# Attention turns of a fused attention and two-MLP kernel in another order

## The chip, the core and the metric

One NeuronCore of a Trainium2 chip. The metric is the device time of one execution in microseconds (us); less is better. The engines named below each run their own list of instructions in order: TensorE (PE; its weight loads are listed apart as PEld), VectorE (DVE), ScalarE (ACT), GpSimd (POOL) and SyncE (SP), which here only issues transfers.

## What is computed

Attention over 4 batches of 12 heads (448 positions of 64 numbers, float32), with q and k normalised by their root mean square and a gain; its result, as 1792 rows of 768, goes through two gated MLPs.

```
def _attn_ref(q, k, v, g_q, g_k):
    q_n, k_n = (rmsnorm(q, g_q), rmsnorm(k, g_k))
    scores = scale * np.matmul(q_n, k_n.transpose(0, 1, 3, 2))
    scores = scores - np.max(scores, axis=-1, keepdims=True)
    attn = np.exp(scores)
    attn = attn / (np.sum(attn, axis=-1, keepdims=True) + 1e-09)
    return np.matmul(attn, v)
...
x = _moe_ref(x)     # (x @ w_a) * (x @ w_b) @ w_out
x = _moe2_ref(x)    # sigmoid(x @ w_gate) * (x @ w_val) @ w_out
```

## The kernel before

Attention takes two heads (a pair) at a time, 24 pairs in all. The work is a software pipeline written out by hand: the tuple `turns` lists steps as (function, offset of the pair, arguments), and a loop over i runs the list once for each turn, every step on pair i + offset. Nothing reorders it: each engine gets its instructions in the order of that list. `begin`, `first` (turn 1) and `end` are such lists for the start and the finish; `turns` runs for i = 2 to 22, 21 times. The MLPs follow, with their own planner, which the change leaves alone; a few of their steps (`decode`, which unpacks weights on ACT and DVE, and `early_hi`, `early_lo`) run inside the turns.

What a turn does, with the names that the trace shows:

- Scores: `s(0, t)`, L350, for t = 0 to 3. Keys and queries are split into a high and a low half (KH, KL, QH, QL), so each score tile is three matmuls. For t = 0, 1, 2 two heads' tiles of 64 rows run side by side, for t = 3 one of 128 rows. Seven score tiles s, in a ring of four PSUM banks.
- Maxima and exponentials: `top`, L356, is the negated row maximum on DVE (tile nm); `exp`, L368, the exponential with the row sum on ACT (tile P, or P3 for t = 3). A score tile's bank is free after its `exp`.
- Turning the exponentials: `x_tr(-1, j, z)`, L378, L381 and for j = 3 L383 to L386, transposes P of the pair of the turn before into a PSUM tile tr. `x_out(-1, j, z)` copies that tile to pt: with z = 0 on ACT (L397, 512 columns, 448 for j = 3), with z = 1 on DVE (L395, 384 columns).
- Value products: `pv(i, part)`, L410, eight matmuls a part, in four concurrent couples, into the one bank pv. Part 0 takes pt of j = 0 and 1, part 1 that of j = 2 and 3; part 1 runs a turn later, as `pv(-2, 1)`. `norm(-2)`, L445 on DVE, then scales pv by the reciprocals rs into xs, and `put` writes xs to DRAM.
- The reciprocals' row: `rsum` on DVE (L417, L418) makes rc; `rsum_tr` (L424) transposes it into a tr tile; `rsum_post` (L429 on ACT, then a transfer from SP) writes it to DRAM; `rsum_get` reads it back three times, spread over partitions, as rs.
- The next pairs' queries and keys: `squares` and `scale` on POOL, `mean` (L239, L253) and `newton` (L268 to L270) on DVE, `rsqrt` on ACT; `t_tr(2, 1)` and `t_tr(2, 0)`, L303 to L308, transpose them into tr tiles; `k_hi` (L323), `k_lo` (L333), `q_hi` (L313), `q_lo` (L318) make the halves; `k_ends` copies 64 columns on POOL.

All tr tiles, ten in a turn, share one ring of three PSUM banks: a tile takes the bank of the one three before it and has to wait until that one was read out.

```
ps_tr = actx.enter_context(tc.tile_pool(name="ps_tr", bufs=3, space=bass.MemoryType.PSUM))
ps_v = actx.enter_context(tc.tile_pool(name="ps_v", bufs=1, space=bass.MemoryType.PSUM))
```

Of the kernel before, what the change touches and what calls it, by code (L numbers as in the profile page):

```python
# [23 lines left out]
def attention_then_two_gated_mlps(  # L24
# [90 lines left out]
    def attention():  # L115
# [269 lines left out]
            for c in range(3):  # L385
                nc.tensor.transpose(tr[:, 64 + P * c:64 + P * c + P], p[c][:, NQ:NQ + P], ident)  # L386

        def x_out(i, j, z):
            d = st[i]
            if z == 0:  # L390
                d["pt"][j] = pt.tile([P, S if j == R else S2], F32, tag=f"pt{j == R}", name="pt", bufs=2 if j == R else 4)
            w = slice(0, S) if j == R else slice(512 * z, S2 if z else 512)
            tr = d.pop(("X", j, z))[:, 0:w.stop - w.start]
            if z:
                nc.vector.tensor_copy(d["pt"][j][:, w], tr)  # L395
            else:
                nc.scalar.copy(out=d["pt"][j][:, w], in_=tr)  # L397
# [102 lines left out]
        def warm(i, n):  # L500
# [17 lines left out]

        first = (
            (s, 0, 0), (x_tr, -1, 0, 0), (x_tr, -1, 0, 1), (s, 0, 1), (top, 0, 0), (x_out, -1, 0, 0), (exp, 0, 0),  # L520
            (top, 0, 4), (exp, 0, 4), (mean, 2), (x_out, -1, 0, 1), (t_tr, 1, 1), (t_tr, 1, 0), (top, 0, 1),
            (k_hi, 1), (load, 4), (load_r, 3), (load_v, 1), (k_lo, 1), (q_hi, 1), (rsqrt, 2), (q_lo, 1), (k_ends, 1),
            (exp, 0, 1), (top, 0, 5), (newton, 2), (scale, 2, 1), (scale, 2, 2), (scale, 2, 0), (s, 0, 2),
            (x_tr, -1, 1, 0), (x_out, -1, 1, 0), (exp, 0, 5), (rsum, -1),
            (x_tr, -1, 1, 1), (x_out, -1, 1, 1), (s, 0, 3),
            (x_tr, -1, 2, 0), (top, 0, 2), (x_out, -1, 2, 0), (exp, 0, 2), (x_tr, -1, 2, 1), (rsum_tr, -1), (top, 0, 6), (exp, 0, 6),
            (x_out, -1, 2, 1), (rsum_post, -1), (pv, -1, 0), (top, 0, 3), (t_tr, 2, 1), (exp, 0, 3), (mean, 3), (rsqrt, 3), (x_tr, -1, 3, 0),
            (k_hi, 2), (newton, 3), (k_lo, 2), (t_tr, 2, 0), (x_out, -1, 3, 0), (q_hi, 2), (q_lo, 2), (k_ends, 2),
        )

        turns = (
            (rsum_get, -2), (early, 0), (put, -3), (s, 0, 0), (s, 0, 1),
            (x_tr, -1, 0, 0), (x_tr, -1, 0, 1), (top, 0, 0), (x_out, -1, 0, 0), (exp, 0, 0), (top, 0, 4),
            (exp, 0, 4), (x_out, -1, 0, 1), (pv, -2, 1), (scale, 2, 1), (scale, 2, 0), (scale, 2, 2), (top, 0, 1),
            (exp, 0, 1), (load, 4), (load_r, 3), (load_v, 1), (x_tr, -1, 1, 0), (top, 0, 5), (rsum, -1), (exp, 0, 5),
            (x_out, -1, 1, 0), (x_tr, -1, 1, 1), (norm, -2), (x_out, -1, 1, 1), (s, 0, 2),
            (s, 0, 3), (decode, 0, 0), (early_hi, -1), (squares, 3), (early_lo, -1), (x_tr, -1, 2, 0),
            (top, 0, 2), (x_out, -1, 2, 0), (exp, 0, 2), (x_tr, -1, 2, 1), (rsum_tr, -1), (top, 0, 6), (exp, 0, 6), (x_out, -1, 2, 1), (rsum_post, -1),
            (pv, -1, 0), (top, 0, 3), (t_tr, 2, 1), (exp, 0, 3), (decode, 0, 1), (mean, 3), (rsqrt, 3), (x_tr, -1, 3, 0),
            (k_hi, 2), (newton, 3), (k_lo, 2), (t_tr, 2, 0), (x_out, -1, 3, 0), (q_hi, 2), (q_lo, 2), (k_ends, 2),  # L540
        )

        end = (
            (close, -1), (rsum_get, -3), (put, -4), (s3, -1, fetch_third, 0), (s, -1, 0), (s, -1, 1),
            (x_tr, -2, 0, 0), (x_tr, -2, 0, 1), (top, -1, 0),
            (exp, -1, 0), (rsum, -2), (x_out, -2, 0, 0), (top, -1, 4), (exp, -1, 4), (x_out, -2, 0, 1), (pv, -3, 1),
            (top, -1, 1), (exp, -1, 1), (x_tr, -2, 1, 0), (top, -1, 5), (x_out, -2, 1, 0), (x_tr, -2, 1, 1),
# [816 lines left out]
    with tc.manual_schedule():  # L1364
        main = mlps()
        attention()
        open_places(6, 4, 2, 3)
        begin_mm("mm1", 2)
        for c in range(KC):
            place(where[0]["A22"], "l", c, F32, "f")  # L1370
        for n, c in (("A22", 0), ("A21", 0), ("A22", 1), ("A21", 1), ("A21", 2), ("A22", 2)):
            stage_in(0, n, c)
        for c in range(KC):
            stage_in(0, "A11", c)
        low_third(1)
        sum_third(2)
        next(main)
        cast_third(2)
        next(main)
        next(main)  # L1380
        low_third(2)
        ready[0] = True
        for _ in main:
            pass
# [29 lines left out]
```

## Time and profile before

| | |
|---|---|
| time, 3 runs | 1216.91 us median (1214.32 to 1217.16) |
| profiled execution | 1218.25 us; span 1216.5 us, 1.75 us around it |
| busy share of the span | PE 98%, PEld 84%, DVE 76%, ACT 54%, POOL 13% |
| chain that ended last, by engine | PE 89%, DVE 5%, DMA 2%, ACT 2% |
| stretch 120 to 150 us: busy of 30 us | PE 30.00, DVE 26.09, ACT 22.98, POOL 17.70; granted clock 1.00 |

The span is the time from the first to the last instruction of the profiled execution. The chain follows the work that ended last back in time, at each step to what released it. A matmul's end is modelled, so a PE that is busy all the time says only that its instructions follow one another closely; where the time goes is read from the distances between starts.

### The profile page before, as it was taken

The numbers are of one execution on the slowest core, as the hardware profiler recorded it, in microseconds if no ns is written. First come the engines' busy times: TensorE is split into PE (matmuls) and PEld (weight loads), VectorE is DVE, ScalarE is ACT, GpSimd is POOL, SyncE is SP. The second block draws the span as 40 slices with busy tenths as digits, with TensorE's granted clock in tenths as the row PEclk, the third lists the DMA queues.
The fourth block names the chain that finished last, engine by engine and source line by source line (L and its number), as shares of the span: only waits on it lengthen the run. The fifth ranks groups of instructions, "written<-read, shape, count | busy, mean of one in ns | idle before, by whom it ended". The sixth has DMA issues, their size and how long they took to land.

```text
span 1216.5 us, 18277 instructions
## 1 busy us (share of the span) xinstructions
PE 1197.6 (98%) x6468; PEld 1016.2 (84%) x6468; DVE 918.7 (76%) x1625; ACT 654.0 (54%) x1276; POOL 157.3 (13%) x241
## 2 busy tenths in 40 slices
PE   8999999999999999999999999999999999999997
PEld 6666666667888888888888888888888888999997
DVE  8888888977858687875768688876786877666672
ACT  7778778864533433444355566534545344445542
POOL 5665668600000000000000000000000000000000
PEclk9999999999999999999999999999999999999999
DMA  5444455348235464654955753234665654777683
GB/s 134 133 141 118 121 149 161 95 147 307 61 113 182 140 204 148 199 187 132 326 183 184 242 178 117 77 125 126 183 194 144 204 160 143 266 254 238 197 258 97
DMA packets 142764, 205.78 MB, mean 169 GB/s; under 512 B 23208, under 2 KB 116560, under 8 KB 142672
## 3 DMA queue, kind: packets, MB, share of 16 engines
q1 hardware_dynamic: 142064, 204.18, 53.5%
q8 instruction: 51, 0.84, 0.3%
q10 hardware_dynamic: 480, 0.43, 0.1%
q14 instruction: 41, 0.34, 0.1%
q0 software_dynamic: 128, 0.00, 0.0%
HBM read 150.21 MB, written 54.35 MB: 168 GB/s over the span
## 4 chain that ended last, share of the span: by engine, by line
PE 89%; DVE 5%; DMA 2%; ACT 2%; issue 1%; POOL 0%; ACTq 0%; SPq 0%; DVEq 0%; POOLq 0%
PE mm L992 46%; PE mm L1275 13%; PE mm L1285 10%; PE pv L410 7%; PE s L350 6%; PE tr L381 4%; PE tr L303 1%; PE tr L378 1%; DVE xl L627 1%; DMA wd<-d 1%; DMA fh<-xd 1%; PE tr L386 1%; DMA xd<-xs 0%; DVE u L1016 0%; DVE al L904 0%
## 5 line engine op out<-in xcount | busy, mean ns | idle before, releaser
L992 PE MATMUL mm<-xl,wh 128*128 128x512 f32 (+1 forms) x1008 | 370.3, 367 | 3.6 <-DVE xl L627 3.6
L992 PE MATMUL mm<-xh,wh 128*128 128x512 f32 (+1 forms) x1008 | 369.6, 367 | 2.4 <-ACT u L1044 2.4
L992 PE MATMUL mm<-xh,wl 128*128 128x512 f32 (+1 forms) x1008 | 371.4, 369 | 0.0
L992 PEld LDWEIGHTS mm<-xl,wh 128*128 128x128 f32 x1008 | 190.6, 189 | 27.6 <-DVE xl L627 4.8
L992 PEld LDWEIGHTS mm<-xh,wh 128*128 128x128 f32 x1008 | 190.7, 189 | 26.8 <-ACT u L1044 2.7
L992 PEld LDWEIGHTS mm<-xh,wl 128*128 128x128 f32 x1008 | 190.4, 189 | 21.1
L627 DVE TENSOR_TENSOR wl<-d,wh 128x384 fp32r<-128x384 f32 x250 | 136.5, 552 | 67.0 <-ACT wh L1152 41.2
L813 ACT CAST wh<-d 128x384 fp32r<-128x384 f32 x166 | 82.0, 514 | 98.1 <-DVE d L801 75.1
L700 DVE SCALAR_TENSOR_TENSOR d<-d,raw 128x384 uint32<-128x384 uint32 x138 | 77.8, 564 | 55.3 <-ACT d L693 49.4
L693 ACT ACTIVATE d<-raw 128x384 f32<-128x384 f32 x138 | 75.6, 553 | 80.6 <-DMA raw<-in_moe_w_out_dram 40.5
L368 ACT ACTIVATE P<-s,nm 128x448 f32<-128x448 f32 x168 | 105.0, 635 | 4.4 <-DVE nm L356 3.6
L1152 ACT CAST wh<-d 128x384 fp32r<-128x384 f32 x84 | 43.2, 514 | 118.3 <-issue 36.8
L356 DVE TENSOR_REDUCE nm<-s 128x1 f32<-128x448 f32 x168 | 97.5, 614 | 3.1 <-PE s L350 3.1
L1285 PE MATMUL mm<-wh,gh 128*128 128x384 f32 x294 | 98.8, 336 | 0.7 <-ACT al L1300 0.4
L1285 PE MATMUL mm<-wl,gh 128*128 128x384 f32 x294 | 98.6, 335 | 0.0
L1285 PE MATMUL mm<-wh,gl 128*128 128x384 f32 x294 | 98.5, 335 | 0.0
L1275 PE MATMUL mm<-gl,wh 128*128 128x512 f32 x252 | 92.6, 368 | 0.0
L1275 PE MATMUL mm<-gh,wl 128*128 128x512 f32 x252 | 92.4, 366 | 0.0
L1275 PE MATMUL mm<-gh,wh 128*128 128x512 f32 x252 | 91.7, 364 | 0.0
L696 DVE SCALAR_TENSOR_TENSOR raw<-raw 128x384 uint32<-128x384 uint32 x140 | 78.4, 560 | 4.0
L397 ACT COPY pt<-tr 128x512 f32<-128x512 f32 x96 | 54.9, 572 | 47.8 <-PE tr L381 45.2
L1062 DVE TENSOR_TENSOR u<-mm,u 128x896 f32<-128x896 f32 x48 | 52.2, 1087 | 30.3 <-PE mm L992 30.2
(161 smaller groups left out, 1947.5 us busy)
## 6 DMA issues: line engine op xcount, KB each, us to landing
gd<-u SPq DMA_DIRECT2D x60, 448.0 KB
u<-gd SPq DMA_DIRECT2D x60, 448.0 KB
d<-wd SPq DMA_DIRECT2D x132, 192.0 KB
raw<-in_moe_w_out_dram SPq DMA_DIRECT2D x48, 384.0 KB
wd<-d SPq DMA_DIRECT2D x72, 192.0 KB
raw<-in_moe_w_a_dram SPq DMA_DIRECT2D x24, 384.0 KB
raw<-in_moe_w_b_dram SPq DMA_DIRECT2D x24, 384.0 KB
raw<-in_moe_w_val_dram SPq DMA_DIRECT2D x23, 384.0 KB
```

Source lines behind the costliest of these rows:

```text
L350: nc.tensor.matmul(out_, w[e, o:o + P], x[e, m:m + S], start=(n == 0), stop=(n == 2))
L356: nc.vector.tensor_reduce(out=d["nm"][:, t:t + 1], in_=d["ps"][t], axis=AX.X, op=ALU.max, negate=True)
L368: nc.scalar.activation(out=e, in_=d["ps"].pop(t), func=AF.Exp, bias=d["nm"][:, t:t + 1], accum_out=d["sum"][:, t:t + 1])
L410: nc.tensor.matmul(d["pv"][64 * h:64 * h + 64], w, x, start=(j == 0), stop=(j == R), skip_group_check=True)
L627: eng.tensor_tensor(out=lo, in0=t, in1=f32(hi), op=ALU.subtract)
L693: nc.scalar.activation(out=f32(t), in_=f32(high), func=AF.Copy, scale=2.0 ** -112)
L696: nc.vector.scalar_tensor_tensor(out=low, in0=high, scalar=0x80000000, in1=low, op0=ALU.bitwise_and, op1=ALU.bitwise_or)
L700: nc.vector.scalar_tensor_tensor(out=t, in0=t, scalar=3, in1=low, op0=ALU.logical_shift_left, op1=ALU.bitwise_or)
L813: nc.scalar.copy(out=hi, in_=t)
L992: nc.tensor.matmul(ps[:, o:o + size], w[:, P * c:P * c + P], x[:, o:o + size], start=(p in (1, 5) and c == 0 and z == 0), stop=(c == KC - ...
L1275: nc.tensor.matmul(ps[:, o:o + size], w[:, P * un:P * un + P], g[:, o:o + size], start=(p in (1, 5) and f == 0 and z == 0), stop=(f == HF ...
L1285: nc.tensor.matmul(ps[:, o:o + HB], g[:, P * t:P * t + P], w, start=(p in (1, 5) and f == 0 and z == 0), stop=(f == HF - 1 and z == 2), sk ...
```

## The change

`turns` is laid out anew, `first` and `end` in the two steps that cross a turn's edge, and `x_out` gets a switch that exchanges its two engines.

- `pv(-2, 1)` stands right behind `s(0, 0)` and `s(0, 1)`, and `pv(-1, 0)` right behind `s(0, 2)` and `s(0, 3)`. The transposes that stood between them come after.
- `rsum`, `rsum_tr` and `rsum_post` move from the end of the turn to its first third; `rsum_get` now runs in the same turn, not at the start of the next.
- `q_lo` moves to the next turn, behind `rsum`.
- `x_out` of j = 2 has its engines exchanged: z = 0 (512 columns) goes to DVE, z = 1 (384 columns) to ACT. Maxima, exponentials and the other copies take other places.

```
@@
-        def x_out(i, j, z):
+        def x_out(i, j, z, swapped=False):
...
-            if z:
+            if bool(z) != swapped:
                 nc.vector.tensor_copy(d["pt"][j][:, w], tr)
@@
-            (k_hi, 2), (newton, 3), (k_lo, 2), (t_tr, 2, 0), (x_out, -1, 3, 0), (q_hi, 2), (q_lo, 2), (k_ends, 2),
+            (k_hi, 2), (newton, 3), (k_lo, 2), (t_tr, 2, 0), (x_out, -1, 3, 0), (q_hi, 2), (k_ends, 2), (rsum_get, -1),
@@
         turns = (
-            (rsum_get, -2), (early, 0), (put, -3), (s, 0, 0), (s, 0, 1),
-            (x_tr, -1, 0, 0), (x_tr, -1, 0, 1), (top, 0, 0), (x_out, -1, 0, 0), (exp, 0, 0), (top, 0, 4),
...
+            (early, 0), (put, -3), (s, 0, 0), (s, 0, 1), (pv, -2, 1), (top, 0, 0), (exp, 0, 0), (top, 0, 4), (exp, 0, 4),
+            (rsum, -1), (q_lo, 1), (rsum_tr, -1), (rsum_post, -1), (scale, 2, 1), (scale, 2, 0), (scale, 2, 2),
...
+            (x_out, -1, 1, 1), (load, 4), (load_r, 3), (load_v, 1), (rsum_get, -1), (s, 0, 2), (s, 0, 3), (pv, -1, 0),
...
+            (x_out, -1, 2, 0, True), (t_tr, 2, 1), (x_out, -1, 2, 1, True), (rsqrt, 3), (x_tr, -1, 3, 0), (k_hi, 2),
@@
-            (close, -1), (rsum_get, -3), (put, -4), (s3, -1, fetch_third, 0), (s, -1, 0), (s, -1, 1),
+            (close, -1), (put, -4), (s3, -1, fetch_third, 0), (s, -1, 0), (s, -1, 1),
```

On PE, in one turn, from the end of `s(0, 1)` to the start of `s(0, 2)` (L410 is `pv`, L378 and L381 are `x_tr`, L424 is `rsum_tr`):

```order
 L350 MATMUL s<-KL,QH 128x448 x2
-L378 MATMUL tr<-ident,P_1361 128x2x64
-L381 MATMUL tr<-ident,P 128x128 x6
 L410 MATMUL pv<-pt,v 64x448 x2
 L410 MATMUL pv<-pt,rz_281 64x448 x2
-L378 MATMUL tr<-ident,P_1361 128x2x64
+L424 MATMUL tr<-ident,rc 7x128
+L378 MATMUL tr<-ident,P_1356 128x2x64
+L381 MATMUL tr<-ident,P 128x128 x6
+L378 MATMUL tr<-ident,P_1356 128x2x64
 L381 MATMUL tr<-ident,P 128x128 x6
 L350 MATMUL s<-KH,QH 128x448 x2
```

Seven transposes left the place ahead of `pv` and stand behind it; with `rsum_tr` that makes 15 transposes in a row.

On PE, in the same turn, from the end of `s(0, 3)` to `t_tr(2, 1)` (L303):

```order
 L350 MATMUL s<-KL,QH 128x448
-L378 MATMUL tr<-ident,P_1361 128x2x64
-L381 MATMUL tr<-ident,P 128x128 x6
-L424 MATMUL tr<-ident,rc 7x128
 L410 MATMUL pv<-pt,v 64x448 x4
+L378 MATMUL tr<-ident,P_1356 128x2x64
+L381 MATMUL tr<-ident,P 128x128 x6
 L303 MATMUL tr<-ident,qkn 128x128 x3
```

Here too the seven transposes went behind `pv`, where the ones of `t_tr` and `x_tr(-1, 3, 0)` follow: 21 in a row.

On DVE, the second half of a turn of before, from the maxima of `s(0, 2)` on:

```order
L356 TENSOR_REDUCE nm<-s 128x1 x2
L395 COPY pt<-tr 128x384
L356 TENSOR_REDUCE nm<-s 128x1
L694 TENSOR_SCALAR raw<-raw 128x384
L239 TENSOR_REDUCE ms<-sq 128x14
L253 TENSOR_SCALAR ms<-ms 128x14
L268 SCALAR_TENSOR_TENSOR t<-y 128x14
```

and a turn's second half of after, in a turn with two steps of `decode` (L696 and L700):

```order
L395 COPY pt<-tr 128x384 x2
L696 SCALAR_TENSOR_TENSOR raw<-raw 128x384
L356 TENSOR_REDUCE nm<-s 128x1 x3
L700 SCALAR_TENSOR_TENSOR d_1697<-d_1697,raw 128x384
L239 TENSOR_REDUCE ms<-sq 128x14
L253 TENSOR_SCALAR ms<-ms 128x14
L395 COPY pt<-tr 128x512
L268 SCALAR_TENSOR_TENSOR t<-y 128x14
```

The copy of `x_out(-1, 2, .)` on DVE moved from between the maxima to behind `mean` (L239, L253), and is the one of 512 columns now.

## Rows read from the trace of the kernel before

**Rows 1.** Chain that ended last: start us, us, what; first and last regular turn

```profile
30.76 1.43 PE s L350 x12
...
245.04 1.42 PE s L350 x12
```

**Rows 2.** Timeline, PE: start us, us, line, op, out<-in, count; one turn

```profile
148.55 0.47 PE L350 MATMUL s<-KH,QH 64*128 64x448 f32 x2
...
149.47 0.37 PE L350 MATMUL s<-KH,QL 64*128 64x448 f32 x2
149.67 0.37 PE L350 MATMUL s<-KL,QH 64*128 64x448 f32 x2
149.97 0.33 PE L378 MATMUL tr<-ident,P 128*128 128x128 f32 x1
150.13 0.82 PE L381 MATMUL tr<-ident,P 128*128 128x128 f32 x6
150.88 0.97 PE L410 MATMUL pv<-pt,v 128*64 128x448 f32 x4
...
152.54 0.33 PE L378 MATMUL tr<-ident,P 128*128 128x128 f32 x1
152.70 0.82 PE L381 MATMUL tr<-ident,P 128*128 128x128 f32 x6
...
154.76 0.36 PE L350 MATMUL s<-KL,QH 128*128 128x448 f32 x1
154.97 0.27 PE L378 MATMUL tr<-ident,P 128*128 128x128 f32 x1
...
155.73 0.27 PE L424 MATMUL tr<-ident,rc 128*7 128x128 f32 x1
155.93 1.72 PE L410 MATMUL pv<-pt,v 128*64 128x448 f32 x8
```

**Rows 3.** Timeline, PE, after the turns: an MLP matmul, then value products

```profile
274.41 0.34 PE L992 MATMUL mm<-xl,wh 128*128 128x384 f32 x1
274.58 0.34 PE L992 MATMUL mm<-xh,wl 128*128 128x384 f32 x1
274.85 0.97 PE L410 MATMUL pv<-pt,v 128*64 128x448 f32 x4
```

**Rows 4.** Timeline, same turn as Rows 2: ACT's first copy, PE's weight loads

```profile
150.66 0.58 ACT L397 COPY pt<-tr 128x512 f32<-128x512 f32 x1 [1.15 <-PE tr L381]
...
152.59 0.69 PEld L381 LDWEIGHTS tr<-ident,P 128*128 128x128 f32 x6
```

**Rows 5.** Timeline near the end: PE waits for a bank that ACT reads

```profile
267.75 0.58 ACT L397 COPY pt<-tr 128x512 f32<-128x512 f32 x1 [0.60 <-PE tr L381]
...
268.39 0.33 PE L378 MATMUL tr<-ident,P 128*128 128x128 f32 x1 [0.29 <-ACT pt L397]
...
268.56 0.49 PE L381 MATMUL tr<-ident,P 128*128 128x128 f32 x3
```

**Rows 6.** Groups by shape, 30 to 255 us: count, busy us, mean ns, idle before

```profile
L395 DVE COPY pt<-tr 128x384 f32<-128x384 f32 x63 | 34.8, 552 | 3.9 <-PE tr L381 3.4
...
L318 DVE TENSOR_TENSOR QL<-tr,QH 128x512 fp32r<-128x512 f32 x21 | 14.5, 692 | 4.7 <-ACT QH L313 4.7
...
L239 DVE TENSOR_REDUCE ms<-sq 128x14 f32<-128x448 f32 x19 | 11.8, 619 | 0.0
...
L700 DVE SCALAR_TENSOR_TENSOR d<-d,raw 128x384 uint32<-128x384 uint32 x8 | 5.4, 680 | 0.0
...
L696 DVE SCALAR_TENSOR_TENSOR raw<-raw 128x384 uint32<-128x384 uint32 x8 | 4.6, 576 | 0.0
```

**Rows 7.** Timeline, DVE, same turn as Rows 2

```profile
151.68 1.14 DVE L356 TENSOR_REDUCE nm<-s 128x1 f32<-128x448 f32 x2
152.74 0.16 DVE L417 TENSOR_SCALAR rc<-sum 128x7 f32<-128x7 f32 x1
...
153.11 0.62 DVE L445 TENSOR_TENSOR xs<-pv,rs 128x448 f32<-128x448 f32 x1
```

More of the change, by code (lines that the diff above doesn't have):

```diff
@@ L534, in attention @@
[L534 to L538, printed above, removed]
@@ L539, in attention @@
-            (pv, -1, 0), (top, 0, 3), (t_tr, 2, 1), (exp, 0, 3), (decode, 0, 1), (mean, 3), (rsqrt, 3), (x_tr, -1, 3, 0),
-            (k_hi, 2), (newton, 3), (k_lo, 2), (t_tr, 2, 0), (x_out, -1, 3, 0), (q_hi, 2), (q_lo, 2), (k_ends, 2),
+            (early, 0), (put, -3), (s, 0, 0), (s, 0, 1), (pv, -2, 1), (top, 0, 0), (exp, 0, 0), (top, 0, 4), (exp, 0, 4),
+            (rsum, -1), (q_lo, 1), (rsum_tr, -1), (rsum_post, -1), (scale, 2, 1), (scale, 2, 0), (scale, 2, 2),
+            (x_tr, -1, 0, 0), (x_out, -1, 0, 0), (top, 0, 1), (exp, 0, 1), (x_tr, -1, 0, 1), (norm, -2),
@@ new lines, in attention @@
+            (x_tr, -1, 1, 0), (x_out, -1, 1, 0), (top, 0, 5), (exp, 0, 5), (x_tr, -1, 1, 1), (x_out, -1, 0, 1),
+            (x_out, -1, 1, 1), (load, 4), (load_r, 3), (load_v, 1), (rsum_get, -1), (s, 0, 2), (s, 0, 3), (pv, -1, 0),
+            (decode, 0, 0), (early_hi, -1), (squares, 3), (early_lo, -1), (top, 0, 2), (exp, 0, 2), (top, 0, 6),
+            (exp, 0, 6), (x_tr, -1, 2, 0), (x_tr, -1, 2, 1), (top, 0, 3), (exp, 0, 3), (decode, 0, 1), (mean, 3),
+            (x_out, -1, 2, 0, True), (t_tr, 2, 1), (x_out, -1, 2, 1, True), (rsqrt, 3), (x_tr, -1, 3, 0), (k_hi, 2),
@@ L541, in attention @@
+            (newton, 3), (k_lo, 2), (x_out, -1, 3, 0), (t_tr, 2, 0), (q_hi, 2), (k_ends, 2),
         )
         end = (
-            (close, -1), (rsum_get, -3), (put, -4), (s3, -1, fetch_third, 0), (s, -1, 0), (s, -1, 1),
+            (close, -1), (put, -4), (s3, -1, fetch_third, 0), (s, -1, 0), (s, -1, 1),
             (x_tr, -2, 0, 0), (x_tr, -2, 0, 1), (top, -1, 0),
```

## The prediction

> **What bounds the kernel now.** I read the chain that ended last first, then the order of the code, then one turn of the timeline engine by engine. In the chain the 21 regular turns are almost nothing but PE: the same six or seven pieces of PE work return with the same period. The first begins at 30.76 us, the last at 245.04 [rows 1]; (245.04 - 30.76) / 20 = 10.714 us a turn, and none of the PE rows of the turn that I opened ends an idle time [rows 2]. So a turn is as long as PE's list, and only two things can change it: the gaps between PE's instructions and new waits of PE. DVE and ACT have free time, but if PE's list gets shorter or tighter, they are the ones to be late.
>
> What a gap is, I read as the distance between starts, less the distance inside a run of equal instructions. Inside the scores a couple starts every 0.20 us (149.47 to 149.67). Six transposes span 0.82, of which the last is 0.27 long: (0.82 - 0.27) / 5 = 0.11 [rows 2].
>
> **The part that shortens PE's list.** Per turn, all from [rows 2]. Removed:
> - scores of 64 rows to transposes: 149.67 to 149.97 is 0.30, so 0.10 over the 0.20; the second transpose comes 0.16 after the first, 0.05 over the 0.11;
> - transposes to value products: the sixth L381 starts at 150.13 + 5 x 0.11 = 150.68, L410 at 150.88: 0.20, so 0.09;
> - value products to transposes: 152.54 to 152.70, 0.05;
> - scores of 128 rows to transposes: 154.76 to 154.97 is 0.21, so 0.01, next to nothing;
> - the row's transpose to value products: 155.73 to 155.93, 0.09.
>
> Sum 0.39. Added: value products to the row's transpose, 0.05 as above, and two direct steps from scores to value products, which the turn of before does not have. The nearest row is an MLP matmul of 128 rows followed by value products: 274.58 to 274.85 is 0.27, where its like is 0.17 apart (274.41 to 274.58), so 0.10 [rows 3]. I take 0.10 for each, since the 64-row scores also left with 0.10. Bounds: free (0), or 0.20 if rows and columns of the array are rearranged one after the other. New sum 0.05 + 0.10 + 0.10 = 0.25. The layout saves 0.39 - 0.25 = 0.14 us a turn, 21 x 0.14 = 2.9 us; with the bounds 0.34 and -0.06 a turn, 7.1 us saved to 1.3 lost.
>
> The rows show 0.09 to 0.10 where the shape of the array's tiles changes and 0.01 where it does not (s of 128 rows to transposes). [...]
>
> **The part that puts waits on PE.** The ten tr tiles of a turn share three banks. Before, value products of 1.66 us (150.88 to 152.54) stand between the transposes, so a bank has long been read when its turn comes. After, 15 and then 21 transposes follow one another, and a bank is wanted again after the seven or eight transposes of two other tiles. Two of these places don't fit. I count from the first transpose of the run; the k-th (k > 1) starts at 0.16 + 0.11 (k - 2).
> - x_tr(1, 1) is the 13th of the first run: due at 1.37, its successor at 1.48. It wants the bank of x_tr(0, 0), which is the 2nd to 5th: the last starts at 0.49 and ends at 0.49 + 0.27 = 0.76. ACT starts 0.04 behind (in the turn of before the last of the four starts at 150.13 + 2 x 0.11 = 150.35, ends at 150.62, the copy starts at 150.66 [rows 4]) and copies for 0.58: 1.38. PE goes on 0.06 after such a copy (267.75 + 0.58 = 268.33, L378 at 268.39), and the next transpose comes 0.17 later (268.56) [rows 5], at 1.38 + 0.06 + 0.17 = 1.61, not 1.48: 0.13 lost.
> - x_tr(3, 0) is the 13th of the second run and wants the bank of x_tr(2, 0), the 1st to 4th: ends at 0.38 + 0.27 = 0.65. That copy is now DVE's and has 512 columns. Before DVE copies 384 columns in 0.55; the nearest row with 512 is L318 with 0.69 [rows 6], which I take. 0.65 + 0.04 + 0.69 + 0.06 + 0.17 = 1.61, not 1.48: 0.13 lost, if DVE is free in time.
>
> All the other tr tiles find their bank read: that of x_tr(1, 0) was the row's tile, 7 rows on ACT; those of the second run, j = 2 and t_tr, hold copies from ahead of the scores; x_tr(0, 1) wants q_lo's bank, which DVE reads two maxima, the reciprocals and 0.69 us into the turn, before PE is through the value products.
>
> A wait holds up the weight load too: in the run the loads start 0.11 ahead of their matmuls (152.59 against 152.70) [rows 2, 4], behind the wait for ACT the second matmul came 0.17 after the first [rows 5], so nothing had been loaded ahead. [...]
>
> So a turn changes by -0.14 + 0.26 = +0.12 us, 21 x 0.12 = 2.5 us.
>
> **What else moves, at no cost, and its cover.** The row (rsum, rsum_tr, rsum_post) comes earlier: its transpose stands behind 1.66 us of value products, while DVE needs two maxima (1.06 from 151.68 to 152.74) and the reciprocals (0.37, to 153.11) [rows 7] after the first scores. On SP the row's transfer and the three of rsum_get are moved past the loads of the next pairs and ahead of the weights' raw transfers; SP waits for ACT's row in both orders. The loads behind it are for pairs one to four turns on, so 10 us cover them; if not, squares on POOL (its list is unchanged) and mean come late, see below. The reciprocals are now wanted by norm a turn later, so their round trip has more time. norm frees the one pv bank between two maxima, several us ahead of the next part 0. q_lo has a turn's time.
>
> **Rivals.**
> - *The waits don't show* (copies end sooner, or weights are loaded ahead): only the layout is left, -2.9 us. For it: each wait is short, 0.07 us ahead of the penalty. Against: the sum of measured rows exceeds what is there at both places.
> - *Scores to value products is free*: then a turn saves 0.20 more. With the waits 2.5 - 4.2 = -1.7 us, without them -7.1. Against it: the 0.10 of [rows 3].
> - *Slower: DVE becomes late for x_tr(2, 0).* Its copy stands behind three maxima, a step of decode and mean, which all come after s(0, 2). Up to there DVE's list from the first scores' end (third couple at 149.67 - 0.60 = 149.07, plus 0.37, plus 0.04, less 148.55: 0.93 into the turn) is 1.06 + 0.37 + 0.69 + 0.53 + 0.62 + 0.53 + 2 x 0.55 = 4.90: 5.83. PE is done with s(0, 2) at 1.42 + 1.66 + the run of 15 (0.16 + 13 x 0.11 + 0.20 + 0.13 = 1.92) + 0.89 = 5.89, so without decode DVE waits for PE there: 5.89 + 0.04 + 3 x 0.53 + 0.62 and mean's short end is some 8.3, while x_tr(2, 0) is ready at 1.42 + 1.66 + 1.92 + 1.61 + 1.66 + 0.65 = 8.9 (1.61: s(0, 2) and s(0, 3) took from 152.70 + 5 x 0.11 + 0.20 = 153.45 to 154.97, 1.52, and leave with 0.09 more). In a turn with L696 and L700 add 0.58 before and 0.68 behind the maxima [rows 6]: 5.83 + 0.58 + 1.59 + 0.68 + 0.62 and the short end, about 9.5: 0.6 late, and PE with it. There are 8 such turns: 8 x 0.6 = 4.8 us, total +7.3. Against it: durations overlap (two maxima of 1.14 together hold DVE for 1.06), and counted by such distances DVE is just in time. It decides from the point where mean ends after 8.9 us of the turn.
> - *That nothing changes at all* is excluded on PE: the order is other, as the listing shows.
>
> **How the numbers follow.** The profiled execution took 1218.25 us, 1.34 above the median of 1216.91; I put differences on the median. Forecast: 1216.91 + 2.5 = 1219.4, +0.2%. A measurement of this kernel tells about 0.3% (3.65 us) from no change, so the bounds are 1213.3 and 1220.6. Cases: the forecast, 50%, of which 12 lie beyond 1220.6 since the two waits may be 0.05 longer; the waits don't show, 22% (1214.0), of which 8 lie below 1213.3; scores to value products free, 10% (1215.2 with the waits, 1209.8 without), of which 4 lie below; DVE late, 18% (up to 1224.2), of which 16 lie above. Faster 8 + 4 = 12%, slower 12 + 16 = 28%, same the other 60%. The range goes from a little below the layout's gain alone, 1213.8, to a DVE that is half as late as by durations in its 8 turns, and waits 0.05 longer: 1219.4 + 2.4 + 1.1, 1223.0.
>
> **What would show it.** The period of the turns: 10.83 by the forecast, 10.57 without waits, 10.37 with a free step besides. PE rows of L381 that end a wait for ACT's L397 (first run), and of L383 that end one for DVE's L395 (second run), 21 each, with starts moved by about 0.07 us. Scores to L410 with 0.10 over the pitch. DVE idle between L253 and the 512-column L395 in turns without decode; if it is not, DVE is late and the period differs from turn to turn. The prediction is wrong if a wait stands anywhere else on PE, above all at s, or if the stretch behind 255 us, which I leave as it is, moves by itself.

## The result, and the profile after

| | before | after |
|---|---|---|
| median | 1217.04 us of 6 runs (1214.32 to 1219.81) | 1223.61 us of 6 runs (1222.65 to 1224.35) |
| profiled execution, span | 1218.25, 1216.5 | 1223.74, 1222.0 |
| busy share PE, DVE, ACT | 98%, 76%, 54% | 98%, 76%, 54% |

The ratio is 1.0061, with a 95% interval of 1.0045 to 1.0076: the kernel became 0.6% slower, 4.2 us more than the forecast and 0.6 us above the upper end of the range.

The chain that ended last of after (start, us, what), the rows that answer to [rows 1]:

```profile
30.67 1.42 PE s L350 x12
...
41.45 1.42 PE s L350 x12
...
69.67 1.42 PE s L350 x11
...
178.07 1.44 PE s L350 x12
...
244.88 1.41 PE s L350 x12
...
265.32 1.42 PE s L350 x11
```

These are starts of the first scores of turns 2, 3, 5, 15 and 21, and of `end`. Before, a turn took 10.714 us throughout; `end` began at 254.77. So the stretches differ by:

| stretch | after | before, at 10.714 a turn | difference |
|---|---|---|---|
| turn 2 | 10.78 | 10.71 | +0.07 |
| turns 3 and 4 | 28.22 | 21.43 | +6.8 |
| turns 5 to 14 | 108.40, 10.84 each | 107.14 | +1.3 |
| turns 15 to 20 (with `early_lo`) | 66.81, 11.14 each | 64.28 | +2.5 |
| `end` begins | 265.32 | 254.77 | +10.55 |
| behind that, to the end of the span | 956.7 | 961.7 | -5.0 |

The ordinary turns are what was forecast, 10.83. The rest was not: one event in turns 3 and 4, six longer turns, and time that comes back behind the turns (with a second profile of before, 2.8 us instead of 5.0; see below).

**The event.** Timeline of after, turn 3, four engines (start us, us, engine, line, operation; in brackets the idle time ahead and what ended it):

```profile
45.04 0.30 SPq L431 DMA_DIRECT2D dr<-row  x1
...
47.81 1.73 SPq L438 DMA_DIRECT2D rs<-dr  x3
49.58 0.59 SPq L682 DMA_DIRECT2D raw<-in_moe_w_a_dram  x1
...
54.49 0.36 DVE L694 TENSOR_SCALAR raw<-raw 128x384 uint32<-128x384 uint32 x1 [5.58 <-DMA raw<-in_moe_w_a_dram]
...
55.49 0.68 DVE L395 COPY pt<-tr 128x512 f32<-128x512 f32 x1
...
54.95 0.46 ACT L397 COPY pt<-tr 128x384 f32<-128x384 f32 x1
...
55.47 0.48 PE L383 MATMUL tr<-swap,P 128*128 128x128 f32 x1 [4.36 <-ACT pt L397]
```

SP waits for the row (45.04), issues four loads, then the three transfers of `rsum_get` (47.81), and only then the first transfer of the MLP's weights into raw (49.58; before it left at 46.70). That transfer lands at 54.49. DVE and ACT stand in `decode` until then. Behind `decode`, ACT copies x_tr(2, 1), 384 columns, until 54.95 + 0.46 = 55.41, and PE's L383 starts 0.06 later. It does not wait for DVE's 512-column copy of x_tr(2, 0), which starts only at 55.49. So the statement ahead of the prediction, that a tile takes the bank of the one three before it, does not hold in every turn: here x_tr(3, 0) took the bank of x_tr(2, 1). The wait for raw was there before as well, on a small scale. From the timeline of before, SP, and from its waits, 30 to 70 us (total us, times, longest):

```profile
46.70 0.46 SPq L682 DMA_DIRECT2D raw<-in_moe_w_a_dram  x1
...
DVE raw L694 <- DMA raw<-in_moe_w_a_dram: 0.7, 1, 0.7
```

So the slack of this transfer was already below zero when the change let it leave 2.9 us later; it also took longer to land, 4.9 us against 3.9 (46.70 to 50.60 in before). The reading back does not explain that: in e10 below, with the same transfers ahead, it took 3.65 (50.72 to 54.37). What does stays open.

While PE waited, its granted clock fell to 0.50. Windows of after (stretch, its length, busy us and instructions of PE, PEld, DVE, ACT, POOL, granted clock, DMA share, GB/s):

```profile
51.00:53.00 2.00, 0.11 (x2) 0.00 (x0) 0.00 (x0) 0.00 (x0) 0.00 (x0) 1.00 0.82 183
53.00:54.00 1.00, 0.00 (x0) 0.00 (x0) 0.00 (x0) 0.00 (x0) 0.00 (x0) 0.64 1.02 353
54.00:60.00 6.00, 4.53 (x21) 3.58 (x21) 3.68 (x10) 3.24 (x8) 2.71 (x6) 0.50 0.15 57
```

**The ordinary turn.** Timeline of after, PE, PEld, DVE and ACT, in one turn (it began at 145.47, the next at 156.37):

```profile
151.67 0.36 PE L350 MATMUL s<-KL,QH 128*128 128x448 f32 x1
151.96 1.73 PE L410 MATMUL pv<-pt,v 128*64 128x448 f32 x8
...
153.78 0.82 PE L381 MATMUL tr<-ident,P 128*128 128x128 f32 x6
...
154.87 0.27 PE L308 MATMUL tr<-ident,qkn 128*64 128x128 f32 x1
155.17 0.33 PE L383 MATMUL tr<-swap,P 128*128 128x128 f32 x1
...
155.16 0.14 PEld L383 LDWEIGHTS tr<-swap,P 128*128 128x128 f32 x1 [0.29 <-ACT pt L397]
...
157.43 0.38 PE L350 MATMUL s<-KL,QH 64*128 64x448 f32 x2
157.74 0.97 PE L410 MATMUL pv<-pt,v 128*64 128x448 f32 x4
...
159.39 0.28 PE L424 MATMUL tr<-ident,rc 128*7 128x128 f32 x1
159.50 0.27 PE L378 MATMUL tr<-ident,P 128*128 128x128 f32 x1
...
160.78 0.31 PEld L381 LDWEIGHTS tr<-ident,P 128*128 128x128 f32 x3 [0.15 <-ACT pt L397]
...
154.44 0.68 DVE L395 COPY pt<-tr 128x512 f32<-128x512 f32 x1
...
154.63 0.48 ACT L397 COPY pt<-tr 128x384 f32<-128x384 f32 x1 [0.38 <-PE tr L381]
```

Both places of the prediction are there. x_tr(1, 1) waits at 160.78 for ACT's copy; L383 comes 0.30 behind L308 instead of 0.11. In most turns it follows DVE's 512-column copy (in the turn before this one the copy ended at 144.20, L383 started at 144.26, and ACT's copy ended only at 144.32). The turn shown is one with a step L700 of `decode`, and here its weight load ends a wait for ACT's copy, as in turn 3: that copy ended at 154.63 + 0.48 = 155.11, DVE's at 154.44 + 0.68 = 155.12. Scores to value products is 0.31 and 0.29, 0.11 and 0.09 over the 0.20.

**The six long turns.** Timeline of after, POOL, DVE and PE, turn 16:

```profile
196.45 2.09 POOL L473 TENSOR_TENSOR xl<-xst,xh 128x896 fp32r<-128x896 f32 x1 [0.50 <-ACT xh L467]
...
197.09 1.48 DVE L253 TENSOR_SCALAR ms<-ms 128x14 f32<-128x14 f32 x1
...
198.48 0.68 DVE L395 COPY pt<-tr 128x512 f32<-128x512 f32 x1
...
199.22 0.33 PE L383 MATMUL tr<-swap,P 128*128 128x128 f32 x1 [0.51 <-DVE pt L395]
```

and of turn 17:

```profile
205.74 1.15 POOL L217 TENSOR_TENSOR sq<-sq 128x448 f32<-128x448 f32 x1
...
205.86 1.45 DVE L696 SCALAR_TENSOR_TENSOR raw<-raw 128x384 uint32<-128x384 uint32 x1
```

L253, mean's second step on 14 columns, takes 1.48 us; it ends with POOL's subtraction of `early_lo`, at 198.57 against 198.54. Apart from POOL's subtraction it takes 0.17. Behind it stands the copy that PE waits for. Five of the six turns are of this kind (L253 takes 0.93 to 1.48). In turn 17 L253 takes 0.18, and it is L696 that takes 1.45 beside POOL's L217, where it takes 0.55 in the ordinary turns; the maxima, mean and the copy stand behind it.

### The profile page after: what moved, and what is told of

It reads as the page before. It is cut to its first block, busy times and chain, and to the rows that moved or that the text cites. A ratio compares the mean times of both kernels' runs of the same rounds, so it can differ in the third digit from the quotient of the medians.

```text
span 1222.0 us, 18340 instructions
## 1 busy us (share of the span) xinstructions
PE 1198.6 (98%) x6468; PEld 1012.6 (83%) x6468; DVE 926.4 (76%) x1625; ACT 658.5 (54%) x1276; POOL 157.1 (13%) x241
## 4 chain that ended last, share of the span: by engine, by line
PE 87%; DVE 7%; DMA 2%; ACT 2%; issue 1%; POOL 0%; SPq 0%; ACTq 0%; DVEq 0%; POOLq 0%
PE mm L992 46%; PE mm L1275 13%; PE mm L1285 12%; PE pv L410 5%; PE s L350 5%; PE tr L381 3%; DVE nm L356 2%; PE tr L303 1%; DVE xl L627 1%; PE tr L378 1%; DVE pt L395 1%; PE tr L386 1%; DVE ms L253 1%; DMA fh<-xd 1%; PE tr L383 1%
## 5 line engine op out<-in xcount | busy, mean ns | idle before, releaser
L992 PE MATMUL mm<-xl,wh 128*128 128x512 f32 (+1 forms) x1008 | 369.1, 366 | 3.5 <-DVE xl L627 3.5
L992 PE MATMUL mm<-xh,wl 128*128 128x512 f32 (+1 forms) x1008 | 370.2, 367 | 0.0
L992 PE MATMUL mm<-xh,wh 128*128 128x512 f32 (+1 forms) x1008 | 368.2, 365 | 1.1 <-ACT u L1044 1.1
L992 PEld LDWEIGHTS mm<-xl,wh 128*128 128x128 f32 x1008 | 189.6, 188 | 27.4 <-DVE xl L627 4.7
L992 PEld LDWEIGHTS mm<-xh,wh 128*128 128x128 f32 x1008 | 189.9, 188 | 25.5 <-issue 1.4
L992 PEld LDWEIGHTS mm<-xh,wl 128*128 128x128 f32 x1008 | 189.5, 188 | 21.0
L693 ACT ACTIVATE d<-raw 128x384 f32<-128x384 f32 x138 | 75.8, 554 | 82.2 <-DMA raw<-in_moe_w_out_dram 41.0
L700 DVE SCALAR_TENSOR_TENSOR d<-d,raw 128x384 uint32<-128x384 uint32 x138 | 76.7, 556 | 52.2 <-ACT d L693 45.9
L696 DVE SCALAR_TENSOR_TENSOR raw<-raw 128x384 uint32<-128x384 uint32 x140 | 79.0, 564 | 4.0
L627 DVE TENSOR_TENSOR gl<-u,gh 128x896 fp32r<-128x896 f32 x60 | 65.1, 1085 | 11.1 <-ACT gh L1189 10.8
```

What stands on the lines that cost most here:

```text
L627: eng.tensor_tensor(out=lo, in0=t, in1=f32(hi), op=ALU.subtract)
L693: nc.scalar.activation(out=f32(t), in_=f32(high), func=AF.Copy, scale=2.0 ** -112)
L696: nc.vector.scalar_tensor_tensor(out=low, in0=high, scalar=0x80000000, in1=low, op0=ALU.bitwise_and, op1=ALU.bitwise_or)
L700: nc.vector.scalar_tensor_tensor(out=t, in0=t, scalar=3, in1=low, op0=ALU.logical_shift_left, op1=ALU.bitwise_or)
L992: nc.tensor.matmul(ps[:, o:o + size], w[:, P * c:P * c + P], x[:, o:o + size], start=(p in (1, 5) and c == 0 and z == 0), stop=(c == KC - ...
```

## Experiments

None of the kernels that follow leaves out any of the work. Ratios are against runs of before on the same chip, whose medians there were 1216.2 to 1217.4.

### One transfer on SP: the event of turn 3

e1_fill_early is the changed kernel with the first raw transfers half a turn earlier, ahead of the row and of the reading back:

```
-            if i > 2 and not (n == 1 and 14 < i < 21):
+            if (i, n) == (2, 1) or i > 2 and (i, n) != (3, 0) and not (n == 1 and 14 < i < 21):
```

> The changed kernel, with the very first transfer of raw weights started half a turn earlier: the first decode step, which only issues it, moves from turn 3's first place to turn 2's second place, and turn 3's first place stays empty, so all later steps keep their places. Theory A (a part of the loss is one event: SP stood behind rsum_get, the first raw transfer left late, ACT waited 4.65 us for it at L693 and PE with it, and the granted clock fell to 0.5 for 6.8 us): no wait of L693 over 1 us in turn 3, no half-clock stretch before 70 us, the two turns from 41.5 us on take 21.7 us and not 28.2, attention ends 6.5 us earlier, and the time falls from 1223.6 to 1217 or 1218; if the MLPs then no longer give back 5 us, to no less than 1220. Rival B (the loss is made by the two bank waits in all 21 turns): the wait moves or goes, the time stays within 1 us of 1223.6.

Measured 1216.51 us (1215.31 to 1218.96), ratio 1.0005 (0.9992 to 1.0018). That is 7.1 us less than after (6.8 by the ratios); turns 3 and 4 took 21.65 us, as theory A told, and rival B is out. The waits of PE in e1, 30 to 255 us, are down to one line, four of the `early_lo` turns:

```profile
PE tr L383 <- DVE pt L395: 1.4, 4, 0.5
```

e2_get_late only moves `rsum_get` behind that transfer:

```
-            (x_out, -1, 1, 1), (load, 4), (load_r, 3), (load_v, 1), (rsum_get, -1), (s, 0, 2), (s, 0, 3), (pv, -1, 0),
-            (decode, 0, 0), (early_hi, -1), ...
+            (x_out, -1, 1, 1), (load, 4), (load_r, 3), (load_v, 1), (s, 0, 2), (s, 0, 3), (pv, -1, 0),
+            (decode, 0, 0), (rsum_get, -1), (early_hi, -1), ...
```

> The changed kernel, with rsum_get moved behind the first decode step of the turn, so that SP issues raw weights first and then reads the reciprocals' row; the loads of the next pairs stay where the change put them, behind SP's wait for the row. Theory A1 (rsum_get alone made the raw transfer late): the first raw transfer leaves some 5 us into turn 3 as in the kernel before, and the wait of 4.65 us at L693 is gone. Theory A2 (the wait for the row and the four loads behind it make most of it): rsum_get's three issues take 1.73 us, so the raw transfer leaves 1.7 us earlier, at about 47.8 us, and 2.9 of the 4.65 us of waiting stay; the clock may still fall. Rival B: no change of time.

Measured 1220.05 us (1218.76 to 1221.89), ratio 1.0035 (1.0022 to 1.0047): half of the event is gone. Raw left at 47.84, and ACT still waited 2.5 us for it (theory A2 told 2.9). The waits of PE in e2, 30 to 70 us:

```profile
PE tr L383 <- ACT pt L397: 2.2, 1, 2.2
```

Here the granted clock stayed at 1.00, and turn 3 took 13.27 us, 2.5 too many. So `rsum_get`'s 1.7 us on SP are about one half; the other is that the loads stand behind the row's wait.

e10_row_no_fill comes from the other side: the order of before, with the row alone moved (the loads stand behind it, as in after), and raw where it was. Its partner e8_row_only, below, has the early raw besides and no event.

> The order of before with the reciprocals' row (and q_lo) alone at its new place, and the weights' first raw transfer where before and the changed kernel have it, in turn 3. Differs from the kernel with the row alone (1214.6, ratio 0.9986) only in that transfer. Theory A (the early row puts its wait, the loads and the reading back ahead of the raw transfer on SP, and that alone makes turn 3 late; the order of PE has no part in it): raw leaves near 50.4 instead of 46.7 us, DVE and ACT wait for it 4 to 6 us, PE waits over 4 us for tr L383, the clock falls to 0.5 for some us, time 1214.6 + 7.1 = 1221.7 (+-1.5), ratio 1.0045. Theory B (the event needs the value products' new places, with transposes behind one another and DVE late): no wait of PE over 1 us in turn 3, time 1214 to 1216.5.

Measured 1220.31 us (1216.22 to 1222.94), ratio 1.0023 (1.0004 to 1.0042), against 0.9986 of e8: +0.37%, some 4.5 us. The event is back without any new place for value products or transposes. The chain of e10 runs through SP (in this kernel the lines behind the list are one higher, L695 is L694 of before):

```profile
48.95 0.45 SPq L438
...
50.72 3.63 DMA raw<-in_moe_w_a_dram
54.37 0.36 DVE raw L695
```

What missed is the size, 7.1 us, and the place: PE waited 3.3 us, at L378 of the next turn, where L383 had been expected, and its granted clock was 0.50 for 3.4 us, where it was so for 6.8 in after. Turns 3 and 4 of the profiled execution (1216.64 us, among its shortest) took 26.30 us, 4.95 more than in e8. That the late transfer makes the event is shown. Its price differs from run to run: e10's ten times lie from 1216.2 to 1222.9.

### L253 beside POOL's subtraction: the six long turns

e3_mean_act is e1 with mean's second step on ACT:

```
-            nc.vector.tensor_scalar(out=ms, in0=ms, scalar1=1.0 / D, scalar2=1e-6, op0=ALU.mult, op1=ALU.add)
+            if i > 3:
+                nc.scalar.activation(out=ms, in_=ms, func=AF.Copy, scale=1.0 / D, bias=1e-6)
+            else:
+                nc.vector.tensor_scalar(out=ms, in0=ms, scalar1=1.0 / D, scalar2=1e-6, op0=ALU.mult, op1=ALU.add)
```

> The earlier first transfer of e1, and mean's second step (L253, 14 numbers a row, times 1/64 plus a constant) from pair 4 on put on ACT instead of DVE. Theory C (in the six turns with early_lo, from 178 to 245 us, DVE's L253 takes 1.48 us beside POOL's L473 instead of 0.17, and so the 512-column copy behind it, and PE's L383, come late): these six turns take 10.85 us and not 11.14, 1.8 us less in all than in e1, and the DVE row of 1.48 us does not appear again. Rival D (those turns are long because ACT's L467 of 0.95 us makes the exponentials late): they stay at 11.1 us or grow, since ACT gets more to do.

Measured 1214.13 us (1212.58 to 1215.72), ratio 0.9983 (0.9971 to 0.9994), 2.4 below e1. No wait of PE is left between 30 and 255 us, and all turns have one length. The chain of e3, turns 5, 15 and 21 (lines three higher):

```profile
63.27 1.41 PE s L353 x12
...
171.01 1.41 PE s L353 x12
...
235.61 1.44 PE s L353 x12
```

10.774 a turn in the first ten and 10.767 in the six, against 10.83 and 11.13 in e1 and the 10.85 that theory C told; rival D is out. So the long turns came from DVE's L253 standing beside POOL's subtraction (in turn 17 L696 no longer stands beside L217 either: it takes 0.56). The alternation of 10.77 and 10.88 in e1's ordinary turns is gone too. In turns with L700 two things came together: L383 waited for ACT's copy, free at 155.11 in the turn shown for after, and DVE was late by about a tenth with its own (the fourth transpose of x_tr(2, 0) starts at 153.78 + 2 x 0.11 = 154.00 and ends 0.27 later, so the copy could have begun at 154.31; it began at 154.44, and ended at 155.12). Either alone would have held PE as long; no run parts them.

### The terms of a turn

e4_no_swap is e1 with the engines of x_out(2, .) not exchanged, so that ACT's 512-column copy frees the bank of x_tr(2, 0): `(x_out, -1, 2, 0)` and `(x_out, -1, 2, 1)` without `True`.

> The earlier first transfer of e1, and the exchange of engines for j = 2 undone: the 512-column copy of x_tr(2, 0) on ACT again, the 384-column one on DVE. Theory E (PE's L383 waits for the bank of x_tr(2, 0), and 0.69 us on DVE behind mean is worse than 0.58 on ACT): the ordinary turns fall by 0.1 to 10.73 us, the six with early_lo to 10.8, the time is 3 to 4 us below e1. Rival F (ACT has no room for the longer copy ahead of rsqrt, so newton and k_lo come late): turns of 10.9 us and more, the time above e1.

Its figures stand in the table below. Theory E holds: the plain turns took 10.67, the time is 2.8 us below e1 (3 to 4 were expected). In the two turns of 10.95 ACT's decode step L693 stood ahead of the copy, which is what rival F feared for all of them.

e5_pv0_back is e1 with the second half of the list as before:

```
-            (pv, -1, 0),
-            (decode, 0, 0), (early_hi, -1), (squares, 3), (early_lo, -1), (top, 0, 2), (exp, 0, 2), (top, 0, 6),
...
+            (decode, 0, 0), (early_hi, -1), (squares, 3), (early_lo, -1), (x_tr, -1, 2, 0),
+            (top, 0, 2), (x_out, -1, 2, 0), (exp, 0, 2), (x_tr, -1, 2, 1), (top, 0, 6), (exp, 0, 6), (x_out, -1, 2, 1),
+            (pv, -1, 0), (top, 0, 3), (t_tr, 2, 1), (exp, 0, 3), (decode, 0, 1), ...
```

> The changed kernel with the weights' first raw transfer half a turn earlier, and the second half of the turn as before: transposes of j = 2 between the scores and the value products of part 0, copies of j = 2 not exchanged. The first half stays as changed. By the terms of the prediction the second run saved nothing by its layout (0.10 out, 0.10 in) and only the first half's 0.14 and its bank wait of 0.13 stay: period 10.714 - 0.14 + 0.13 = 10.70, time that of the kernel without the exchange, 1213.7 +- 1. No wait of L383 on DVE. Rival (the value products right behind the second scores are a gain of their own): period above 10.77, time 1215 to 1217.

e6_pv1_back is the reverse, with the first half as before, the row's transpose behind the value products:

```
-            (early, 0), (put, -3), (s, 0, 0), (s, 0, 1), (pv, -2, 1), (top, 0, 0), (exp, 0, 0), (top, 0, 4), (exp, 0, 4),
...
+            (x_tr, -1, 0, 0), (x_tr, -1, 0, 1), (top, 0, 0), (x_out, -1, 0, 0), (exp, 0, 0), (top, 0, 4), (exp, 0, 4),
+            (q_lo, 1), (x_out, -1, 0, 1), (rsum, -1), (pv, -2, 1), (rsum_tr, -1), (rsum_post, -1),
```

> The reverse: first half of the turn as before (transposes of j = 0 ahead of the value products of part 1, the row's transpose behind them), second half as changed, copies of j = 2 exchanged; first raw transfer half a turn earlier. By the terms: no gain of the first half, no wait of x_tr(1,1) on ACT, the wait of 0.13 on DVE's 512-column copy stays: period 10.714 + 0.13 = 10.85, time 1216.5 to 1217.5, and the six turns with early_lo longer by 0.3 to 0.4 as in the other kernels with the exchange. Rival (the switch from scores to value products is what costs, not the bank): no L383 wait in the list, yet a period over 10.8.

e7_first_half is e5 with x_tr(0, 1) ahead of x_tr(0, 0), so that the bank of x_tr(1, 1) is read by DVE's shorter and earlier copy:

```
-            (x_tr, -1, 0, 0), (x_out, -1, 0, 0), (top, 0, 1), (exp, 0, 1), (x_tr, -1, 0, 1), (norm, -2),
+            (x_tr, -1, 0, 1), (top, 0, 1), (x_out, -1, 0, 1), (x_tr, -1, 0, 0), (x_out, -1, 0, 0), (exp, 0, 1), (norm, -2),
```

> First half of the turn as changed but with x_tr(0,1) ahead of x_tr(0,0), so that the bank which x_tr(1,1) wants was read by DVE's 384-column copy; second half as before; first raw transfer half a turn earlier. By the terms only the layout's gain is left: period 10.714 - 0.14 = 10.57, 21 x 0.10 = 2.1 us below the kernel without the exchange: 1211.6. Rival (the gain of the layout is not there, the bank wait was smaller than priced): period 10.67, 1213.7. Second rival: DVE's maxima, now one copy earlier in line, make the exponentials late: period over 10.7, with PE waits at s.

e8_row_only is e6's first half and e5's second half: the row, its reading back and `q_lo` have moved, and with them the loads, which stand behind the row as in after; t_tr(2, 0) and the copy of x_tr(3, 0) are exchanged.

> The order of before with one part of the change alone: the reciprocals' row (rsum, its transpose, the copy, the transfer and the reading back) and q_lo at their new places, rsum_get in the same turn and out of the end; value products, transposes and copies stay; first raw transfer half a turn earlier. Tests where the time behind the turns comes from that the three kernels with the early transfer gave back (about 3 us: fh<-xd 6.7 us against 8.1, the MLP's first 144 matmuls 29.6 against 31.1 us). Theory G (the row's earlier reading frees SP's queue at the end): period 10.71 to 10.76, fh<-xd 6.7 and time 1213 to 1214.5. Theory L (it belongs to the order of the value products, or is the luck of one profiled run): same period, 1216 to 1217.5.

| kernel | median us (lowest to highest) | ratio (interval) | us a turn, 5 to 14 | 15 to 20 |
|---|---|---|---|---|
| before, two profiles | 1217.04 (1214.32 to 1219.81) | 1 | 10.71; 10.75 | 10.72; 10.75 |
| e1 | 1216.51 (1215.31 to 1218.96) | 1.0005 (0.9992 to 1.0018) | 10.83 (10.77 and 10.88) | 11.13 |
| e4 | 1213.71 (1212.81 to 1215.66) | 0.9982 (0.9968 to 0.9997) | 10.73 (10.67, two of 10.95) | 10.75 |
| e5 | 1212.73 (1211.01 to 1214.73) | 0.9968 (0.9955 to 0.9981) | 10.65 | 10.67 |
| e6 | 1218.99 (1217.23 to 1220.15) | 1.0027 (1.0015 to 1.0040) | 10.85 (10.79 and 10.90) | 11.22 |
| e7 | 1210.94 (1207.73 to 1212.36) | 0.9955 (0.9937 to 0.9974) | 10.51 | 10.62 |
| e8 | 1214.60 (1211.80 to 1215.46) | 0.9986 (0.9976 to 0.9996) | 10.67 | 10.67 |

The periods are differences of starts in the chain, as of e7:

```profile
62.58 1.42 PE s L350 x12
...
167.71 1.42 PE s L350 x12
...
231.40 1.43 PE s L350 x12
```

and in e7 the row of transposes in which PE had waited runs through. Timeline of e7, PE:

```profile
149.68 0.28 PE L424 MATMUL tr<-ident,rc 128*7 128x128 f32 x1
149.80 0.49 PE L381 MATMUL tr<-ident,P 128*128 128x128 f32 x3
...
150.56 0.27 PE L378 MATMUL tr<-ident,P 128*128 128x128 f32 x1
150.67 0.82 PE L381 MATMUL tr<-ident,P 128*128 128x128 f32 x6
```

The transposes start about 0.11 apart throughout; x_tr(1, 1), the last three of the six, starts at 150.67 + 3 x 0.11 = 151.00, without a wait.

The differences give the terms one by one. The wait for ACT's copy is e5 less e7, 0.14. The wait for DVE's 512 columns is the plain turns of e1 (or e3) less those of e4, 10.77 - 10.67 = 0.10. The layout of the first half without its wait is e7 against before, 10.51 - 10.71 = -0.20 (-0.24 against the second profile of before); the second half adds nothing (e5 and e4's plain turns are alike, 10.65 and 10.67). The row alone (e8) is -0.04, about as much as the two profiles of before differ, so it is only suggested; it is contained in the -0.20. The periods of e5, e7 and e8 came out 0.04 to 0.06 below what was expected, e6's time 1.5 us above it, and e8's time 0.1 above what theory G expected; the other periods and times of e5 to e8 met it.

### The stretch behind the turns

Before needed 961.7 us from the first scores of `end` to the end of the span, and 959.5 in a second profile; e8 needed 959.0, after and e1 to e7 955.7 to 958.8, e9 (below) 958.6, e10 955.8. A difference stands where PE waits for the first MLP tile of `fh`. Behind the first value products of the MLP's start, the waits of PE, 250 to 350 us, in before:

```profile
PE mm L992 <- ACT u L1044: 2.4, 1, 2.4
```

and in after:

```profile
PE mm L992 <- ACT u L1044: 1.1, 1, 1.1
```

e1 to e7 and e9 waited 0.3 to 1.2, e8 2.0. b2_before_again is the kernel before, unchanged:

> The same once more, for the spread. Theory S: wait of 2.0 us or more for L1044 and the clock's fall near 303 us. Theory L: the two looks differ from each other in this wait.

It took 1217.1 us; the wait was 2.3, and the granted clock fell to 0.50 right behind it. A window of this second profile of before, with the granted clock at 0.50:

```profile
304.00:306.00 2.00, 2.00 (x6) 1.52 (x6) 2.00 (x3) 0.58 (x2) 0.00 (x0) 0.50 0.00 0
```

The next 144 matmuls of L992 took 31.16 us there, 31.14 in the first profile and 31.12 in e8, but 29.59 in after:

```profile
294.53 6.68 DMA fh<-xd
...
310.91 29.59 PE mm L992 x144
```

So about 1.3 us of wait and 1.5 us of clock come back behind the turns. It is not the luck of one run, since both profiles of before and e8 show the long wait and the fall, and the nine profiles of orders with value products moved show neither. Theory G, that the row's earlier reading alone does it, falls with e8's wait and clock. But e10, e8's near twin, waited 1.7 us and kept its clock, so the place of the value products doesn't settle it either. Why the transfers of this stretch land later in the old order (`fh<-xd` 8.10 us in before, 6.68 in after, 7.0 to 7.5 in e5, e6 and e10) stays open, and so does the rest of the 5.0.

A further run of before was an execution of 4131.69 us, in which a transpose (L381, 60 to 255 us) took 643 ns on average where it takes 272; it can't be compared.

### A version that beats both

e9_first_half_mean is e7 with e3's edit.

> The kernel with the first half laid out anew and x_tr(0,1) ahead of x_tr(0,0), with mean's second step on ACT instead of DVE from pair 4 on. If the step beside POOL's subtraction is all that makes six turns longer there (their L253 took 0.55 to 1.00 us), the mean period falls from 10.55 to 10.51 and the time by 0.8 us, to 1210.1 +- 1. If ACT is now late with its square root or its copies, PE waits for tr L383 or s and the time is 1211.5 or more.

Measured 1209.80 us (1208.41 to 1211.88), ratio 0.9938 (0.9918 to 0.9958); e7 had 0.9955 (0.9937 to 0.9974). Both are faster than before, by about half a per cent. The turns of e9 took 10.51 and 10.55, those of e7 10.51 and 10.62. The edit takes 0.4 us of the turns, half of what was expected, and the intervals of the two kernels overlap: that it brings something beyond e7 isn't shown.

## Why the prediction was wrong, point by point

**What bounds the kernel**: right. PE's list and its waits set the turn's length in all versions, and what decides are gaps and new waits.

**The layout, -0.14**: the gain is there, its size was -0.19 to -0.20. Scores to value products cost 0.11 and 0.09, as the 0.10 of [rows 3] said; the rival that it is free is refuted. The bound of 0.20 was an estimate of the author's; the 0.11 and 0.09 speak against it. The 0.05 put down for value products to the row's transpose, read as there from the first transpose to the second, is not there: 159.39 to 159.50 is the plain 0.11.

**The two bank waits, 0.13 each**: both there, at the places named, 0.14 and 0.10 (in turns with L700 the second is for another bank than the one named). The estimate of 0.69 for DVE's copy was 0.68. The rival that the waits don't show is refuted by e7 and e4.

**Their sum, 10.83 a turn**: measured 10.84, but that is in part luck, since two errors cancel in it. By the sizes measured a plain turn is 10.71 - 0.19 + 0.24 = 10.76, as in e3 (10.77; the sizes are differences of these same periods, so this is no separate test). The rest is the 0.11 by which every second turn, those with L700, is longer.

**DVE late for x_tr(2, 0)**: the rival was half right. It decides by the end of mean, as told, and it came to 0.1 in turns with L700, not 0.6 (with ACT's copy holding PE as long). In the turns with `early_lo` it came to 0.4 on average, for a reason that the prediction didn't have: in five of the six L253 stood beside POOL's subtraction, with the copy that PE wants right behind it. Before, it started in the turn shown here as the subtraction ended; in four of the six turns it overlapped it and took 0.29 to 0.92 us, but no such copy stood behind it and PE waited for nothing. So too in e4: L253 takes 0.93 to 1.32 us there, and those turns are 10.75. Timeline of before, POOL and DVE:

```profile
187.69 2.11 POOL L473 TENSOR_TENSOR xl<-xst,xh 128x896 fp32r<-128x896 f32 x1
...
189.72 0.17 DVE L253 TENSOR_SCALAR ms<-ms 128x14 f32<-128x14 f32 x1
```

In turn 16 of after the step on 14 columns ended with the subtraction, 198.57 against 198.54, 1.31 us late. Why it takes longer beside POOL the runs do not show; that it did so in five of the six turns (0.93 to 1.48 us), and that all six take 10.77 without it on DVE (e3), they do. The prediction weighed no move of a DVE step to a place beside POOL's subtraction.

**SP's moves, at no cost**: this step failed, and it alone puts the time outside the range. It said that the row's transfer and the three of `rsum_get` move past the loads and ahead of the raw transfers, and named as cover that "10 us cover them". That holds for the loads, which serve pairs one to four turns on. For raw, which serves `decode` in the same half turn, it gave no cover at all; the row of before that shows DVE waiting 0.7 us for it is not among its rows. Turn 3 of the two timelines gives the cost on SP: the first load left at 45.44, behind the wait for the row, where before it left at 43.41, 2.0 later; an idle stretch of 0.9 between the loads of before is gone; the three transfers of `rsum_get`, now between loads and raw, take 1.8. So raw left 2.9 later, and with the 0.7 that makes a wait of some 3.6 us on DVE, once, where the prediction had nothing. It was 5.6 there, 4.4 on PE, and with the clock 6.8 in the two turns. Without this one transfer the kernel is where it was (e1, 1216.5 us, inside the range). That is still 2.9 below the forecast: the six long turns, some 1.8 more than ordinary ones, and the time that came back behind the turns were not in the sum either, and partly cancel.

**The stretch behind 255 us, left as it is**: it moved, by some -3 to -5 us. The prediction named this as something that would make it wrong. Why it moved is open in part (above). With it the sum closes in the two profiled executions: 10.55 later at `end`, less 5.0, is the 5.5 by which the spans differ; the medians differ by 6.6.

## What to carry to other kernels

When steps move on a queue, take every transfer behind them by itself and ask who waits for it and with how much slack; the wait of 0.7 us in the trace of before showed a transfer without any. In turn 3 one late transfer held DVE for 5.6 us, ACT for 4.65 and, by the copy behind `decode`, PE for 4.4; in turn 16 a step beside POOL's subtraction took 1.31 longer, and PE waited 0.51 for the copy behind it. So it seems better to put a copy that frees a bank ahead of steps that depend on DRAM or that may stand beside such a subtraction. When a run of transposes goes through a few banks, let the first tile be the one with the shortest and earliest copy: here that exchange, with its copy (e5 to e7), was worth 0.14 us a turn.

## What the runs showed of the hardware that was not expected

- A 14-column step of DVE took 1.48 us beside a 2.09 us subtraction of POOL, and 0.17 apart from it, and a step on 384 columns 1.45 beside a POOL instruction of 1.15 us instead of 0.55, while mean's reduction (L239), which began with the same subtraction, kept its 0.60 us.
- PE's granted clock fell to 0.50 within a wait of 4.4 us (after), right behind one of 3.3 us (e10) and of 2.0 to 2.4 us (before twice, e8), but not with one of 2.2 us in e2. It stayed at 0.50 for 3.4 us (e10) to 6.8 us (after). The wait of 2.2 us cost 2.5, that of 4.4 us 6.8: what a wait on PE cost here is not read from its length alone.
